# A gated linear attention followed by a squared-ReLU MoE: units of 256 tokens with two adjacent tokens per partition

## The chip, the cores and the metric

The kernel runs on one core of a Trainium2 chip. The metric is the device time of one execution in microseconds (us), lower is better. The kernel before was given at 212.42 us (median of 3, 212.36 to 215.28). Every later comparison runs both kernels in the same rounds on the same chip, and its ratio uses runs in the fast state alone.

## The reference, cut to what matters

```python
# B, H, S, D = 4, 8, 768, 48; q, k, v, alpha: [B, H, S, D] fp32, alpha in [0.8, 1.0]
for t in range(S):
    state = alpha[:, :, t, :, None] * state + einsum('bhd,bhe->bhde', k[:, :, t], v[:, :, t])
    y[:, :, t] = einsum('bhd,bhde->bhe', q[:, :, t], state)
x = y.transpose(0, 2, 1, 3).reshape(B * S, H * D)      # 3072 tokens x 384
h = x @ w_in                                           # 384 x 2048
out = maximum(h, 0) ** 2 @ w_out                       # 2048 x 384, fp32
```

Both kernels compute the recurrence in blocks: a cumulative sum of log(alpha) inside the block (a matmul with a triangular matrix), exponentials that scale k and q, transposes of the scaled k and q, masked scores between tokens of the block, products of the scores with v, and one state per batch entry that is carried from block to block. Then y is transposed and goes through the two layers.

Of the kernel before, what the change touches and what calls it, by code (L numbers as in the profile page):

```python
# [11 lines left out]
class Op:  # L12


    __slots__ = ("eng", "fn", "cost", "prio", "deps", "idx", "lag", "sem", "start", "end", "pos", "name",
                 "users", "ndeps", "alts")

    def __init__(self, eng, fn, cost, prio, name):
        self.eng, self.fn, self.cost, self.prio, self.name = eng, fn, cost, prio, name
        self.deps = {}  # L20
        self.lag = 0
        self.sem = None
        self.users = []
        self.pos = None


class Program:


    HOP = 90  # L30

    def __init__(self, nc):
        self.nc = nc
        self.ops = []
        self.writer = {}
        self.readers = {}
        self.dma_sems = {}
        self.dma_count = {}

    def add(self, eng, fn, cost, prio, reads=(), writes=(), name="", dma=None, lag=0, after=()):  # L40
        op = Op(eng, fn, cost, prio, name)
        op.idx = len(self.ops)
        op.lag = lag
        if dma is not None:
            if dma not in self.dma_sems:
                self.dma_sems[dma] = self.nc.alloc_semaphore("d_" + dma)
                self.dma_count[dma] = 0
            self.dma_count[dma] += 1
            op.sem = (dma, self.dma_count[dma])
        for o in after:  # L50
            op.deps[o] = True
        for k in reads:
            w = self.writer.get(k)
            if w is not None:
                op.deps[w] = True
            if k[0] == "ps":
                for r in self.readers.get(k, ()):
                    if r.eng != eng:
                        op.deps[r] = True
        for k in writes:  # L60
# [3 lines left out]
            for r in self.readers.get(k, ()):  # L64
                if r is not op:
                    op.deps.setdefault(r, r.eng != eng or r.sem is not None)
# [9 lines left out]
    def schedule(self):  # L76

        import heapq
# [4 lines left out]
        free = {}  # L83
        ready = {}
# [3 lines left out]
        for op in self.ops:  # L88
            free.setdefault(op.eng, 0.0)
            ready.setdefault(op.eng, [])  # L90
            if op.ndeps == 0:
                heapq.heappush(events, (0.0, seq, "r", op))
                seq += 1
        avail = {e: [] for e in free}
        order = {e: [] for e in free}
        done = 0
        now = 0.0
        while done < len(self.ops):
            t, _, kind, op = heapq.heappop(events)
            now = t  # L100
            batch = [(kind, op)]
            while events and events[0][0] <= now + 1e-9:
                _, _, k2, o2 = heapq.heappop(events)
                batch.append((k2, o2))
            for k2, o2 in batch:
                if k2 == "r":
                    heapq.heappush(avail[o2.eng], (o2.prio, o2.idx, o2))
            for e in avail:
                while avail[e] and free[e] <= now + 1e-9:
                    _, _, o = heapq.heappop(avail[e])  # L110
                    o.start = now
                    o.end = now + o.cost
                    free[e] = o.end
                    o.pos = len(order[e])
                    order[e].append(o)
                    done += 1
                    land = o.end
                    if o.sem is not None:
                        dma_free = max(dma_free, o.end + 1100) + o.lag
                        land = dma_free + 800  # L120
                    for u in o.users:
                        u.ndeps -= 1
                        hop = self.HOP if u.deps[o] else 0
                        u.start = max(getattr(u, "start", 0.0) or 0.0, land + hop)
                        if u.ndeps == 0:
                            heapq.heappush(events, (max(u.start, now), seq, "r", u))
                            seq += 1
                    heapq.heappush(events, (free[e], seq, "f", o))
                    seq += 1
        self.order = order  # L130
        self.makespan = max(o.end for o in self.ops)

    def place(self):

# [12 lines left out]
        for o in seq:  # L147
            kn = known.setdefault(o.eng, {})
            want = {}
            for d, sync in o.deps.items():  # L150
                if not sync or (o.eng == "pe" and d.eng == "pe" and d.sem is None):
# [6 lines left out]
            ds = sorted(want.values(), key=lambda d: -d.start)  # L158
            mine = []
            for d in ds:  # L160
# [14 lines left out]
        for e, ops in self.order.items():  # L175
# [9 lines left out]
    def emit(self, handles):  # L185
# [28 lines left out]
def pe_ns(*cols):  # L214
    return sum(max(n / 2.4 + 3, 27) for n in cols)


def act_ns(n):
    return 190 + n * 0.8333


def dve_ns(n, rate=1.0):
    return 135 + n / 0.96 / rate


def bass_gla_recurrent__then__act_relu_squared_kernel(
# [13 lines left out]
    C = 128  # L240
    NCH = S // C
# [3 lines left out]
    DP = 64  # L245
    G = B * NCH
    chunks = [(b, c) for c in range(NCH) for b in range(B)]

    NRAW, NLAB, NASB, NQKS, NKQT, NPM, NV, NXB, NRR, NGT, NOSB = 5, 2, 3, 3, 3, 2, 4, 2, 4, 6, 3
# [4 lines left out]
    RAW = sb("raw", [128, 4, HD], FP32, NRAW)  # L254
    LAB = sb("lab", [128, H, DP], BF16, NLAB)
    ASB = sb("asb", [128, 2, HD], BF16, NASB)
    QKS = sb("qks", [128, 2, H, DP], BF16, NQKS)
    KQT = sb("kqt", [128, 2, NPR, 128], BF16, NKQT)
    PM = sb("pm", [128, 2, NPR, 128], BF16, NPM)
    VBF = sb("vbf", [128, HD], BF16, NV)  # L260
    SBD = sb("sbd", [128, HD], BF16, B)
    TMP = sb("tmp", [128, HD], FP32, 2)
    ACM = sb("acm", [128, 2 * NPR], FP32, 2)
    XBF = sb("xbf", [128, HD], BF16, NXB)
    XT = nc.alloc_sbuf_tensor("xt", [128, KT, G * C], BF16)
    LTRI = nc.alloc_sbuf_tensor("ltri", [128, 128], BF16)
# [3 lines left out]
    HCOL = nc.alloc_sbuf_tensor("hcol", [128, 2 * NPR], BF16)  # L270
    WIN = nc.alloc_sbuf_tensor("win", [128, KT, DFF], BF16)
    WOUT = nc.alloc_sbuf_tensor("wout", [128, FT, DM], BF16)
    GT = sb("gt", [128, FT, 2 * C], BF16, NGT)
    RR = sb("rr", [128, 512], BF16, NRR)
    OSB = sb("osb", [128, DM], FP32, NOSB)

    psH = [nc.alloc_psum_tensor(f"psH{i}", [128, 512], FP32) for i in range(2)]
    psP = nc.alloc_psum_tensor("psP", [128, 2, 512], FP32)
    psO = nc.alloc_psum_tensor("psO", [128, 512], FP32)
    psA = nc.alloc_psum_tensor("psA", [128, 512], FP32)  # L280
    psT = nc.alloc_psum_tensor("psT", [128, 1024], BF16)
    psY = nc.alloc_psum_tensor("psY", [128, 512], FP32)
# [3 lines left out]
    P = 7000.0  # L286
# [9 lines left out]
    def fill(buf, val):  # L296
        return lambda e: e.memset(buf[:], val)

    def select(buf, op, fill_v, base, pattern, mult):
        return lambda e: e.affine_select(out=buf[:], in_=buf[:], compare_op=op, fill=fill_v, base=base,  # L300
                                         pattern=pattern, channel_multiplier=mult)

    for i, t in enumerate(LAB):
        add("dve", fill(t, 0.0), 300, -1e6, writes=[("lab", i)])
    for i, t in enumerate(QKS):
        add("dve", fill(t, 0.0), 600, -1e6, writes=[("qks", i)])
    add("pool", fill(LTRI, 1.0), 200, -1e6, writes=[("ltri",)])
    add("pool", select(LTRI, ALU.is_ge, 0.0, 0, [[1, 128]], -1), 300, -1e6, reads=[("ltri",)], writes=[("ltri",)])
    add("pool", fill(ONES2, 1.0), 100, -1e6, writes=[("ones",)])

    for buf, key in ((HSEL, "hsel"), (HCOL, "hcol")):
        add("dve", fill(buf, 0.0), 100, -2e6, writes=[(key,)])
    for part, key, val in ((HSEL[0:1, 64:128], "hsel", -1000.0), (HSEL[32:33, 0:64], "hsel", -1000.0),
                           (HCOL[0:1, 0:2 * NPR:2], "hcol", 1.0), (HCOL[32:33, 1:2 * NPR:2], "hcol", 1.0)):
        add("dve", lambda e, part=part, val=val: e.memset(part, val), 100, -2e6, reads=[(key,)], writes=[(key,)])

    add("pool", fill(IDENT, 0.0), 200, -1e6, writes=[("ident",)])
    add("pool", select(IDENT, ALU.not_equal, 1.0, 0, [[-1, 128]], 1), 300, -1e6, reads=[("ident",)],
        writes=[("ident",)])
    for i in range(B):  # L320
        add("pool", fill(SBD[i], 0.0), 400, -1e6 + 1, writes=[("sbd", i)])
# [4 lines left out]
    WQ = 2  # L326
    FQ = FT // WQ

    def w_in_dma(i):
        src = moe_w_in.rearrange("(kk p) n -> p kk n", p=128)[:, :, i * FQ * 128:(i + 1) * FQ * 128]  # L330
        return lambda e: e.dma_start(WIN[:, :, i * FQ * 128:(i + 1) * FQ * 128], src)

    def w_out_dma(i):
        src = moe_w_out.rearrange("(kk p) n -> p kk n", p=128)[:, i * FQ:(i + 1) * FQ, :]
        return lambda e: e.dma_start(WOUT[:, i * FQ:(i + 1) * FQ, :], src)

    raw_dma = {}
    wi_dma, wo_dma = {}, {}
    W_IN_AFTER = (0, "a")
    LOADS_HELD, W_OUT_AFTER = 1, 4  # L340

    def held(g):
        out = [wi_dma[0]] if g >= LOADS_HELD else []
        return out + ([wo_dma[0]] if g > W_OUT_AFTER else [])

    def attention(g):
        b, c = chunks[g]
        t0 = c * C
        p0 = g * P
        r, la, a, qs, kt, pm, vb, xb = (g % n for n in (NRAW, NLAB, NASB, NQKS, NKQT, NPM, NV, NXB))  # L350
        first, last = c == 0, c == NCH - 1

        for j, t, nm in ((3, alpha, "a"), (0, k, "k"), (1, q, "q"), (2, v, "v")):
            src = t[b, :, t0:t0 + C, :].rearrange("h p d -> p h d")
            dst = RAW[r][:, j, :].rearrange("p (h d) -> p h d", h=H)
# [214 lines left out]
```

## The kernel before: what the change and the argument touch

The kernel describes its work as operations with an engine, a cost, a priority and the buffers that they read and write. A small scheduler orders them per engine ahead of time, and waits on semaphores are derived from the buffers. All times in the code are plan costs in ns.

```python
C = 128                                   # tokens of a block ("chunk"); 24 chunks
RAW = sb("raw", [128, 4, HD], FP32, NRAW) # one token per partition
psA = nc.alloc_psum_tensor("psA", [128, 512], FP32)     # cumulative sums, alone in its bank
psT = nc.alloc_psum_tensor("psT", [128, 1024], BF16)    # every transpose
psY = nc.alloc_psum_tensor("psY", [128, 512], FP32)
...
for j, t, nm in ((3, alpha, "a"), (0, k, "k"), (1, q, "q"), (2, v, "v")):
    src = t[b, :, t0:t0 + C, :].rearrange("h p d -> p h d")       # pieces of 48 fp32 = 192 B
    dst = RAW[r][:, j, :].rearrange("p (h d) -> p h d", h=H)
...
dst = GT[gt][:, u * per:(u + 1) * per, 0:n]
eng, cost = ("pool", 1250) if u % 2 else ("dve", dve_ns(512, 2))  # squares: fixed alternation
...
add("sp", lambda e, ob=ob, r0=r0: e.dma_start(out[r0:r0 + C, :], OSB[ob][:]), 70, ps_ + 1300,
    reads=[("osb", ob)], name=f"out{g}", dma=f"o{ob}", lag=600)   # 128 rows of 1,536 B
```

All loads, outputs and (after the change) transposes by DMA are issued by SyncE into one queue; only the weights go through GpSimd's.

## Time and profile before

| | before |
|---|---|
| time, median | 212.42 us |
| TensorE busy share of the span | 85% |
| the busiest other engines (VectorE, ScalarE) | 52% |
| first 52 us | TensorE busy 24.6 us, DMA share 1.00 (179 GB/s) |
| from 52 us to the end | TensorE busy, nearly without a gap |
| last TensorE end to the end of the span | 209.8 to 212.6: 2.8 us |

The prediction below shows the page, the stretches and the timeline of this kernel. One more view matters later, the page's count of DMA packets and its list of DMA issues. The columns of the list are what was moved, the queue, the number of transfers, the size of one, and the median time in us from issue to landing.

```profile
DMA packets 106197, 27.04 MB, mean 127 GB/s; under 512 B 100288, under 2 KB 105408, under 8 KB 106176
...
raw<-in_k_dram SPq DMA_DIRECT2D x24, 192.0 KB, 3.7
...
raw<-in_alpha_dram SPq DMA_DIRECT2D x24, 192.0 KB, 3.6
out_dram<-osb SPq DMA_DIRECT2D x24, 192.0 KB, 2.3
```

A load of 192 KB lands after 3.6 to 3.7 us, and an output of the same size after 2.3 us.

### The profile page before, as it was taken

The numbers are of one execution on the slowest core, as the hardware profiler recorded it, in microseconds if no ns is written. First come the engines' busy times: TensorE is split into PE (matmuls) and PEld (weight loads), VectorE is DVE, ScalarE is ACT, GpSimd is POOL, SyncE is SP. The second block draws the span as 40 slices with busy tenths as digits, with TensorE's granted clock in tenths as the row PEclk, the third lists the DMA queues.
The fourth block names the chain that finished last, engine by engine and source line by source line (L and its number), as shares of the span: only waits on it lengthen the run. The fifth ranks groups of instructions, "written<-read, shape, count | busy, mean of one in ns | idle before, by whom it ended". The sixth has DMA issues, their size and how long they took to land.

```text
span 212.6 us, 4663 instructions
## 1 busy us (share of the span) xinstructions
PE 180.8 (85%) x1940; PEld 136.0 (64%) x1940; DVE 111.0 (52%) x175; ACT 111.5 (52%) x237; POOL 85.8 (40%) x105
## 2 busy tenths in 40 slices
PE   0346271677999999999999999999999999999984
PEld 0236151565776787777876877868778777677752
DVE  4151360345545767487677555675665655833200
ACT  2204230450665587574675585765756857374540
POOL 4403600140442296282564552735626615033330
PEclk9999855576999999999999999999999999999999
DMA  7499999999989987847907839365041010110101
GB/s 140 61 190 210 215 181 194 194 207 197 215 183 194 232 169 160 187 109 153 223 18 174 181 60 221 92 142 122 3 111 40 0 40 37 39 40 0 40 37 74
DMA packets 106197, 27.04 MB, mean 127 GB/s; under 512 B 100288, under 2 KB 105408, under 8 KB 106176
## 3 DMA queue, kind: packets, MB, share of 16 engines
q1 hardware_dynamic: 103296, 23.60, 51.7%
q0 software_dynamic: 2880, 3.15, 9.5%
q8 instruction: 15, 0.25, 0.4%
q14 instruction: 6, 0.05, 0.1%
HBM read 25.17 MB, written 4.72 MB: 141 GB/s over the span
## 4 chain that ended last, share of the span: by engine, by line
PE 77%; DMA 11%; SPq 6%; DVE 3%; ACT 1%; issue 1%
PE psO L512 30%; PE psH L490 29%; DMA raw<-in_alpha_dram 7%; SPq L356 6%; PE psT L396 4%; DMA win<-in_moe_w_in_dram 4%; PE psP L408 4%; PE psY L424 2%; PE psT L459 2%; PE psA L364 2%; PE psY L421 2%; PE psY L437 1%; DVE qks L386 1%; PE psA L368 1%; ACT osb L519 1%
## 5 line engine op out<-in xcount | busy, mean ns | idle before, releaser
L500 POOL TENSOR_TENSOR gt<-rr 128x512 bf16<-128x512 bf16 x48 | 51.4, 1072 | 73.2 <-ACT rr L496 73.2
L496 ACT ACTIVATE rr<-psH 128x512 bf16<-128x512 f32 x96 | 57.3, 597 | 45.0 <-PE psH L490 43.0
L490 PE MATMUL psH<-xt,win 128*128 128x256 bf16 (+1 forms) x624 | 78.3, 275 | 0.5 <-DMA win<-in_moe_w_in_dram 0.4
L512 PE MATMUL psO<-wout,gt 128*128 128x384 bf16 x384 | 77.6, 330 | 0.7 <-ACT osb L519 0.6
L490 PEld LDWEIGHTS psH<-xt,win 128*128 128x128 bf16 x624 | 58.3, 103 | 10.7 <-issue 0.8
L512 PEld LDWEIGHTS psO<-wout,gt 128*128 128x128 bf16 x384 | 34.0, 98 | 17.8 <-ACT osb L519 1.2
L413 DVE TENSOR_TENSOR pm<-psP,ltri 128x1024 bf16<-128x1024 f32 x24 | 29.3, 1221 | 14.2 <-PE psP L408 13.9
L500 DVE TENSOR_TENSOR gt<-rr 128x512 bf16<-128x512 bf16 x48 | 24.1, 503 | 21.2 <-ACT rr L496 20.7
L386 DVE TENSOR_TENSOR qks<-raw,asb 128x768 bf16<-128x768 f32 x24 | 24.6, 1024 | 17.1 <-ACT asb L377 17.1
L383 POOL CAST vbf<-raw 128x384 bf16<-128x384 f32 x24 | 13.4, 557 | 35.1 <-PE psY L437 18.1
L465 DVE COPY xt<-psT 128x384 bf16<-128x384 bf16 x24 | 8.6, 357 | 28.9 <-PE psT L459 28.9
L364 PE MATMUL psA<-lab,ltri 128*128 128x384 bf16 x24 | 8.4, 349 | 16.4 <-ACT lab L360 16.4
L360 ACT ACTIVATE lab<-raw 128x384 bf16<-128x384 f32 x24 | 12.7, 528 | 17.9 <-DMA raw<-in_alpha_dram 17.9
L402 DVE COPY kqt<-psT 128x1024 bf16<-128x1024 bf16 x24 | 16.5, 689 | 9.5 <-PE psT L396 9.1
L396 PE MATMUL psT<-ident,qks 128*128 128x128 bf16 x192 | 15.7, 229 | 4.7 <-DVE qks L386 4.4
L453 POOL TENSOR_TENSOR sbd<-tmp,acm 128x384 bf16<-128x384 f32 x16 | 15.8, 986 | 8.8 <-DVE tmp L451 8.8
L431 ACT ACTIVATE xbf<-psY 128x384 bf16<-128x384 f32 x24 | 11.8, 493 | 12.8 <-PE psY L424 12.8
L375 ACT ACTIVATE asb<-psA 128x384 bf16<-128x384 f32 x24 | 11.7, 489 | 11.7 <-PE psA L368 10.7
L396 PEld LDWEIGHTS psT<-ident,qks 128*128 128x128 bf16 x192 | 12.8, 102 | 7.2 <-DVE qks L386 5.0
L519 ACT ACTIVATE osb<-psO 128x384 f32<-128x384 f32 x24 | 11.8, 492 | 10.6 <-PE psO L512 10.5
L364 PEld LDWEIGHTS psA<-lab,ltri 128*128 128x128 bf16 x24 | 2.4, 98 | 17.7 <-ACT lab L360 17.1
L408 PE MATMUL psP<-kqt 64*128 64x128 bf16 x192 | 10.2, 230 | 2.6 <-DVE kqt L402 2.6
(36 smaller groups left out, 112.8 us busy)
## 6 DMA issues: line engine op xcount, KB each, us to landing
raw<-in_k_dram SPq DMA_DIRECT2D x24, 192.0 KB, 3.7
raw<-in_q_dram SPq DMA_DIRECT2D x24, 192.0 KB, 3.7
raw<-in_v_dram SPq DMA_DIRECT2D x24, 192.0 KB, 3.7
raw<-in_alpha_dram SPq DMA_DIRECT2D x24, 192.0 KB, 3.6
out_dram<-osb SPq DMA_DIRECT2D x24, 192.0 KB, 2.3
win<-in_moe_w_in_dram POOLq DMA_DIRECT2D x2, 768.0 KB, 9.3
wout<-in_moe_w_out_dram POOLq DMA_DIRECT2D x2, 768.0 KB, 11.3
```

The costliest lines, as they stand in the source:

```text
L364: ins = pe.matmul(psA[:, 0:HD], LTRI[:], lab)
L386: add("dve", lambda e: e.tensor_tensor(QKS[qs][:, :, :, 0:D], RAW[r][:, 0:2, :].rearrange("p j (h d) -> p j h d", h=H), ASB[a][:, :, :].re ...
L396: ins = pe.matmul(psT[:, o:o + 128], QKS[qs][:, j, 2 * p:2 * p + 2, :].rearrange("p h d -> p (h d)"), IDENT[:], is_transpose=True)
L402: add("dve", lambda e: e.tensor_copy(KQT[kt][:].rearrange("p j n s -> p (j n s)"), psT[:, :]), dve_ns(1024, 2), p0 + 3000, reads=[("ps", " ...
L408: ins = pe.matmul(psP[:, h, p * 128:(p + 1) * 128], KQT[kt][64 * h:64 * h + 64, 0, p, :], KQT[kt][64 * h:64 * h + 64, 1, p, :])
L413: add("dve", lambda e: e.tensor_tensor(PM[pm][:].rearrange("p j n s -> p (j n) s"), psP[:, :, :].rearrange("p j (n s) -> p (j n) s", n=NPR ...
L453: add("pool", lambda e: e.tensor_tensor(sb3, TMP[g % 2][:].rearrange("p (n d) -> p n d", d=D), acm, ALU.mult), 1100, p0 + 8000, reads=[("t ...
L490: ins = pe.matmul(psH[hb][:, i * n:(i + 1) * n], WIN[:, kk, fj * 128:(fj + 1) * 128], XT[:, kk, g0 * C:g0 * C + n], start=(kk == 0), stop= ...
L496: add("act", lambda e, hb=hb, rb=rb: e.activation(RR[rb][:], psH[hb][:], AF.Relu), act_ns(512), pu + 600, reads=[("ps", "H", hb)], writes= ...
L500: add(eng, lambda e, rb=rb, dst=dst: e.tensor_tensor(dst, RR[rb][:].rearrange("p (i s) -> p i s", i=per), RR[rb][:].rearrange("p (i s) -> ...
L512: ins = pe.matmul(psO[:, 0:DM], GT[gt][:, fj, ti * C:(ti + 1) * C], WOUT[:, fj, :], start=(fj == 0), stop=(fj == FT - 1))
L519: add("act", lambda e, ob=ob: e.activation(OSB[ob][:], psO[:, 0:DM], AF.Copy), act_ns(DM), ps_ + 700, reads=[("ps", "O")], writes=[("osb", ...
```

## The change

The intent is to shorten the starved start (larger DMA pieces, fewer logarithms, dummy matmuls on zeros that are to keep the clock up), and to take work from TensorE (transposes of the later units by DMA). Each partition now holds two adjacent tokens, so a load piece is 384 B. The product of the two alphas is taken first, and one logarithm serves the pair. The scheduler may now choose between engines for several operations. The diff is long; this is its core, with cuts marked.

```diff
-    C = 128
-    NCH = S // C
+    T = 256
+    NST = S // T
...
+    PE_TRANSPOSED = 6          # units 0 to 5 transpose on TensorE, 6 to 11 by DMA
+    PE_X = 6
+    AHEAD = 1                  # a unit's front is given priority one unit early
...
-    psP = nc.alloc_psum_tensor("psP", [128, 2, 512], FP32)
-    psA = nc.alloc_psum_tensor("psA", [128, 512], FP32)
-    psT = nc.alloc_psum_tensor("psT", [128, 1024], BF16)
-    psY = nc.alloc_psum_tensor("psY", [128, 512], FP32)
+    psX = nc.alloc_psum_tensor("psX", [128, 2, 512], FP32)
+    psZ = nc.alloc_psum_tensor("psZ", [128, 2, 512], FP32)
+    psW = nc.alloc_psum_tensor("psW", [128, 512], FP32)
...
-            src = t[b, :, t0:t0 + C, :].rearrange("h p d -> p h d")
+            src = t[b, :, t0:t0 + T, :].rearrange("h (p j) d -> p h (j d)", j=2)
...
+        add("dve", lambda e: e.tensor_tensor(hd(PRD[la][:]), al(0), al(1), ALU.mult), dve_ns(HD), p0,
+            reads=[("raw", r, 0)], writes=[("prd", la)], name=f"pr{g}",
+            alts={"pool": (lambda e: e.tensor_tensor(...), pool_ns(HD))})
...
+                ins = pe.matmul(psW[:, 0:HD], (LINC if incl else LSTR)[:], LAB[la][:, :, 0:D])
...
+                add("sp", lambda e, dst=dst, src=src: e.dma_start_transpose(dst, src), 500, p0 + 2500 + a,
+                    reads=[("qks", qs, a)], writes=[("kqt", kt, a)], name=f"tr{a}_{g}", dma=f"t{a}_{kt}", lag=1100)
...
+        if g < PE_X:
+            bank = as_bf16(psW)
+            def xtr(pe): ...   # 6 transposes of xbf into bank
+            add("pe", xtr, pe_ns(6, 128), p0 + 6700, reads=[("xbf", x2), ("ident",)], writes=[("ps", "W")],
+                name=f"xt{g}")
...
-            r0 = b * S + c * C
-            add("sp", lambda e, ob=ob, r0=r0: e.dma_start(out[r0:r0 + C, :], OSB[ob][:]), 70, ps_ + 1300,
+            r0 = b * S + i * T + 128 * jq
+            dst = bass.AP(tensor=out.tensor, offset=out.offset + r0 * DM, ap=[[DM, 2], [2 * DM, 64], [1, DM]])
+            add("sp", lambda e, ob=ob, dst=dst: e.dma_start(dst, OSB[ob][:]), 400, ps_ + 1300,
...
+    ORDER = ["f0", "f1", "b0", "b1", "f2", "b2", "f3", "f4", "b3"]     # fronts and backs of units
+    for g in range(5, G):
+        ORDER += [f"f{g}", f"b{g - 1}"]
...
+    pr.fill(lambda pe: pe.matmul(psO[:, 0:512], ZERO[:, 0:128], ZERO[:], skip_group_check=True), 216,
+            min(o.start for o in pr.order["pe"] if o.name.startswith("s2_")), 300, zero)
```

Two of these lines will matter most. The first is the output's access pattern. The rows of an output tile now lie in the order even tokens, odd tokens, so the pattern on the DRAM side has three dimensions, and the outermost has size 2. The second is that the cumulative sums of a unit (its "front") and the later transposes of another unit (its "back") write the same PSUM bank, psW.

## The prediction

> **What bounds the kernel now.** I read the page first, then stretches of ten microseconds, then the timeline. The page, with its slices (5.3 us each) and its chain that ended last:
>
> ```profile
> span 212.6 us, 4663 instructions
> PE 180.8 (85%) x1940; PEld 136.0 (64%) x1940; DVE 111.0 (52%) x175; ACT 111.5 (52%) x237; POOL 85.8 (40%) x105
> ...
> PE   0346271677999999999999999999999999999984
> ...
> PEclk9999855576999999999999999999999999999999
> DMA  7499999999989987847907839365041010110101
> ...
> PE 77%; DMA 11%; SPq 6%; DVE 3%; ACT 1%; issue 1%
> ```
>
> TensorE carries 77% of the chain, no other compute engine exceeds 52%, and everything on the chain that isn't TensorE sits early: PE is 0 to 7 tenths busy in the first ten slices and 9 afterwards. So there are two regimes. The stretches (us, busy time, instructions, clock, DMA share, GB/s) give the border:
>
> ```profile
> 20.00:30.00 10.00, 3.49 (x42) 2.43 (x43) 4.20 (x5) 3.89 (x10) 3.81 (x5) 0.75 1.14 199
> 30.00:40.00 10.00, 3.32 (x34) 2.66 (x33) 1.57 (x3) 1.08 (x3) 0.51 (x1) 0.50 1.16 187
> ...
> 52.40:210.00 157.60, 156.19 (x1687) 116.76 (x1685) 91.44 (x140) 96.29 (x204) 72.86 (x79) 1.00 0.50 111
> ```
>
> After 52.4 us PE is busy 156.2 of 157.6 us at full clock: pure TensorE throughput. Before it the DMA engines are full (share over 1), the compute engines are nearly idle, and the clock falls to half. The timeline shows what was waited for and how densely matmuls issue later:
>
> ```profile
> 31.40 6.04 SPq L356 DMA_DIRECT2D raw<-in_q_dram  x1
> ...
> 38.70 0.52 ACT L360 ACTIVATE lab<-raw 128x384 bf16<-128x384 f32 x1 [9.30 <-DMA raw<-in_alpha_dram]
> ...
> 133.68 1.47 PE L490 MATMUL psH<-xt,win 128*128 128x256 bf16 x12
> 135.08 0.40 PE L408 MATMUL psP<-kqt 64*128 64x128 bf16 x8
> 135.41 1.48 PE L490 MATMUL psH<-xt,win 128*128 128x256 bf16 x12
> 136.73 0.33 PE L364 MATMUL psA<-lab,ltri 128*128 128x384 bf16 x1
> ```
>
> A page's "mean ns" of a matmul (273) includes latency. The pitch is what counts: 135.41 to 136.73 is 1.32 us for 12 matmuls of 256 columns, 109 ns each. From starts in the same stretch: 384 columns 162 ns, 128 columns 56 ns, 96 columns 41 ns, anything under about 50 columns 25 ns. Score matmuls (64 rows) start in pairs 3 ns apart, one pair per 57 ns, so both row halves run together; around them the array stands for 95 ns on each side.
>
> Per 128 tokens before: the two MoE layers 24 x 109 + 16 x 162 = 5.21 us; cumulative sum 0.30; transposes 8 x 56 = 0.45; scores 4 x 57 + 2 x 95 = 0.42; state and intra products 0.17 + 0.21; state update 0.17; later transposes 0.17. Sum 7.10 us. The chain's L490 bursts return every 14.2 us for 256 tokens (133.84, 148.04, 162.24), exactly two of these. Over 24 chunks that is 170.4 us, less 1.9 for what first and last chunks skip: 168.5. So 44 of 212.6 us are no array work at full speed: about 40 in the first 52 us, 2.8 after the last matmul, 1 waiting for the last psO eviction.
>
> [...]the 98,304 packets of 192 B took 15.7 ns each (96 us over 16 engines, 196 GB/s), the 1,536 B output packets 65.5 ns (375 GB/s). [...]
>
> **The change part by part**, per unit of 256 tokens on TensorE.
> - Cumulative sums: one with the state extras (0.16 + 5 x 0.025) and one strict (0.16): 0.45 instead of 0.60.
> - Scores: 32 matmuls of 128 columns, four 64x64 tiles at once: 8 x 57 = 0.46, the same array time as before (two at once over twice the rows). No gain. Two groups, each with a switch in and out: 0.38, as before.
> - Intra products 16 pairs x 25 ns = 0.40 (before 0.42), state 8 x 41 = 0.33 (0.34) and update 0.33 (0.34) are unchanged in time, since halves run in pairs. But they now change mode too: 4 x 95 = 0.38 more.
> - First transposes 16 x 56 = 0.90 and later ones 0.34: unchanged in units 0 to 5, gone from PE in units 6 to 11 (-1.24).
> - MoE 10.42, unchanged.
>
> So units 0 to 5 cost 14.2 - 0.15 + 0.38 = 14.4 us, units 6 to 11 13.2. Sum 6 x 14.4 + 6 x 13.2 = 165.6, less 1.9 for what first and last units skip: 163.7 against 168.5. The steady state gains only 5 us.
>
> Other engines, per unit, by durations from the page. ScalarE: one logarithm 0.53, three exponentials 1.47, the small one 0.19, eight relus 4.78, two evictions of 0.49 and a wide one of about 0.83: 8.8. VectorE: scaling 2 x 1.02, masks 2 x 1.22, two state additions 1.10 and half of the squares 2.0: 7.6, plus about 1.9 for evictions in units 0 to 5. GpSimd: four products of 0.99, one cast of about 1.0, half of the squares 4.3: 9.2. All under 13.2, so none becomes the bound on average, but with less slack than before; a dependency chain of a unit stays hidden while the front is built one unit ahead.
>
> Startup, the larger part. Adjacent tokens make load pieces of 384 B. A line through 192 B at 15.7 ns and 1,536 B at 65.5 ns puts 384 B at 22.8 ns (an estimate): 272 GB/s, and 5.8 us for one 256-token unit (4 x 1,024 pieces) instead of 8.0 for two chunks. The weights took 9.6 (win) and 10.4 us (wout) of all engines and stay. First data at 2.4 us, then units 0 and 1 (11.6) and both weights (20.0): all landed by 34 us, unit 2's alpha by about 36. One unit's chain from alpha to xt is the product 0.55, log 0.53, sums 0.7, exponentials 1.5, scalings 2.0, transpose and eviction 1.7, score and two masks 2.9, products 0.7, evictions 2.0, transpose 0.5, and some sixteen handovers of about 0.1: 15 us. MoE of unit 2 can start near 52 us. Until then PE has units 0 and 1 complete (28.4) and the attention of unit 2 (3.6): 32 of 52 us, 20 lost, against 40 before. The dummy matmuls on zeros until the first second-layer matmul keep the clock up, so that the work there costs its full-speed price; before it cost nearly double from 25 to 45.5 us. One thing runs against this: while wout moved before (27 to 36 us), the 192 B loads got only 5 to 37 GB/s. Unit 1 may be starved in the same way behind win; loads of units 2 and on are now held until wout parts land, so unit 2 comes at about the same time and I charge 2 us.
>
> Tail: the same psO handover and output, 3.8, plus about 0.5.
>
> Sum: 163.7 + 20 + 2 + 4.3 = 190. A scheduler which fits the measured pitches (its switch cost is the 95 ns seen here) probably spends some of unit 2's latency on unit 3's front: I take 188.
>
> **Rivals.**
> (a) Small tiles cost more than their column count: [...]32 score weights and 16 state weights of 64 columns might queue one behind another at about 50 ns (an estimate: half the 97 ns recorded for a load). 32 x 50 - 460 = 1.1 us per unit and 0.4 for state: 18 us, total near 206. Against it: row-tiled weight loads in the old trace start 4 ns apart and overlap.
> (b) DMA transposes as the bound. They enter a single in-order queue on SyncE with the loads and outputs. At 4 us each, three per unit, they'd come to 12 us beside 13.2 and delay xt and kqt: 5 to 10 us more, total 193 to 198. For it: SPq issues already took 6 us when the queue was full. Against it: from unit 6 on the loads are almost done (DMA share under 0.3 from 150 us).
> (c) Static choice of engines and thinner buffers (XBF, EK, EQ, LAB two each) make PE wait where it never did: each 0.5 us per unit is 6 us, total 194.
> (d) Startup better than reckoned: 184 to 181, if unit 2's front overlaps well and weights beat my line.
>
> **Range and chances.** The floor is the 163.7 of array work plus about 13 of unavoidable start and 4 of tail, 181. (b) and (c) together reach 199, (a) 206. To miss 2% (208.2) two rivals have to come true at once. I say 188, 181 to 199; faster 0.94, same 0.04, slower 0.02.
>
> **What would show it.** Right: 4-tile groups pitched at 57 ns; load packets near 23 ns; the clock at full from a few us on; PE dense from about 30 to 35 us instead of 52; total PE pitch of a late unit about 13.2 us. Wrong: weight loads of the score tiles one behind another (a), PE idle released by DMA xt or kqt in the second half (b), PE idle released by VectorE, ScalarE or GpSimd after 60 us (c), or the first MoE block still starting after 40 us because unit 1's loads starve.

## The result, and the profile after

| | before | after |
|---|---|---|
| median, same rounds | 213.85 us (212.36 to 215.51, 4 runs) | 221.76 us (220.89 to 221.82, 4 runs) |
| ratio of fast runs, 95% interval | | 1.037 (1.029 to 1.045): slower |
| span of the profiled run | 212.6 us | 220.1 us |
| last TensorE end to the end of the span | 2.8 us | 9.2 us |

A ratio here is the mean time of one kernel's fast runs over that of the other's of the same rounds, so it is not quite the ratio of the medians. The prediction was 188 us, with 181 to 199. The kernel came out slower by 3.7%, so both the range and the direction were wrong.

The page of the changed kernel, its busy times, slices (5.5 us each) and chain:

```profile
span 220.1 us, 5346 instructions
...
PE 192.9 (88%) x2317; PEld 130.2 (59%) x2317; DVE 135.5 (62%) x214; ACT 101.7 (46%) x186; POOL 58.4 (27%) x72
...
PE   7999999998984998799319999999999999999830
...
PEclk9999999999998599999965999999999999999995
DMA  6997699999466679556979983457915650400110
...
PE 63%; DVE 13%; DMA 13%; SPq 3%; issue 2%; ACT 2%; DVEq 0%
```

TensorE is busy from the first slice (partly with dummy matmuls) and the clock is full (granted 1.0) from 5.5 us to the first dip, as intended. (The first record of the clock in this trace is at 5.5 us. The PEclk digits before a trace's first record are filled in and not measured: until 5.5 us the dummies start 427 ns apart, afterwards 216.) New are two dips, near 70 us and from 107 to 118 us, where PE falls to 4, 3 and 1 tenths and the clock to 0.5 (from 70.4 to 77.2 and from 111.3 to 121.6 us), and the last slices, 8, 3 and 0. TensorE's share of the chain fell from 77% to 63%, and VectorE's rose from 3% to 13%.

The stretches give the same in numbers. The columns are length, then the busy time and instructions of PE, PEld, DVE, ACT and POOL, then the granted clock, the DMA share and GB/s:

```profile
0.00:52.40 52.40, 49.81 (x569) 29.86 (x570) 38.18 (x61) 22.21 (x40) 23.10 (x37) 1.00 0.99 224
52.40:104.00 51.60, 45.14 (x604) 31.83 (x603) 39.94 (x60) 26.93 (x53) 18.23 (x18) 0.93 0.68 186
104.00:130.00 26.00, 17.97 (x192) 11.78 (x191) 11.12 (x18) 9.66 (x20) 5.66 (x6) 0.80 0.94 154
```

Before, PE was busy for 156.2 of the 157.6 us after 52.4. Now it is idle 8 of the 26 us from 104 to 130 alone, and that with a DMA share of 0.94 and only 154 GB/s: the DMA engines are occupied, but they move little.

Busy time also counts latency (a matmul of L658 is 274 ns long on the page, and they start 109 ns apart) and dummies. For a balance I counted each matmul by its steady pitch at full clock (the prediction's pitches). Everything else, dummies, waits, a low clock and the stops of about 95 ns where the tile shape changes (in the kernel before 93 and 94 ns around the scores at 135.1 us), is time without array work:

| time without array work, us | before | after |
|---|---|---|
| 0 to 52 us | 39.2 | 24.1 |
| 52 to 130 us | 4.1 | 25.0 |
| 130 us to the last TensorE end | 3.4 | 6.1 |
| from there to the end of the span | 2.8 | 9.2 |
| array work in the whole span | 163.1 | 155.7 |
| sum: the span | 212.6 | 220.1 |

So the start did win 15 us and the array work shrank by 7, and 21 us were given back between 52 and 130 us, 3 later on and 6 at the end.

The list of DMA issues answers to the one shown of before (loads are 384 KB now, twice as large):

```profile
raw<-in_alpha_dram SPq DMA_DIRECT2D x12, 384.0 KB, 6.0
...
out_dram<-osb SPq DMA_DIRECT2D x24, 192.0 KB
...
kqt<-qks SPq DMA_TRANSPOSE x12, 4.4
```

The output line has lost its landing time: the program could not pair issues with landings. The packet records say why. Outputs are packets of 1,536 B, 128 to a store. In the kernel before, the 128 packets of a store start within 0.6 to 2 us (the first store's within 3.4), and up to 21 of this size are in flight at once. In the changed kernel those of one store are spread over 3.9 to 4.9 us, there are never more than 4 in flight, and the last four stores lie back to back from 200.1 to 218.4 us. A single packet took nearly as long as before (mean 70.7 ns, before 65.5). 64 packets of 65.5 ns one after another are 4.2 us. This is what two DMA engines with 64 packets each would give. The profile does not name the engine of a packet, so "two" is inferred from this and from the pattern of the store; e9 below adds a count that says the same.

The end of the timeline (start, length, engine, line, operation, in brackets the idle time before it and what ended it):

```profile
210.93 0.49 ACT L690 ACTIVATE osb<-psO 128x384 f32<-128x384 f32 x1 [2.87 <-PE psO L683]
```

The last tile leaves PSUM at 211.4 us, and the span ends at 220.1. The 8.7 us between are stores that are still queued.

And the dip at 107 to 118 us:

```profile
108.35 0.99 POOL L447 TENSOR_TENSOR prd<-raw 128x384 f32<-128x384 f32 x1 [8.33 <-DMA raw<-in_alpha_dram]
109.30 1.04 POOL L673 TENSOR_TENSOR gt<-rr 128x512 bf16<-128x512 bf16 x1
110.48 0.81 PE L683 MATMUL psO<-wout,gt 128*128 128x384 bf16 x4 [3.85 <-POOL gt L673]
115.47 0.64 PE L573 MATMUL psX<-kqt 64*64 64x128 bf16 x16 [4.18 <-DMA kqt<-qks]
```

A late load of alpha holds GpSimd for 8.33 us. GpSimd works in its fixed order, so a square that was ready stands behind it. TensorE waits 3.85 us for this square, and a little later 4.18 us for a transpose by DMA. This is why a late DMA for another unit reaches TensorE. SyncE, which issues all of these in order, is held up too: it took 4.95 us to issue one transpose at 104.1 us, and 27.5 us for all twelve transposes `kqt<-qks`, where in e1 below it took at most 2.14 and in total 17.0 us.

### The profile page after: what moved, and what is told of

It is laid out like the page before. It is cut to its first block, busy times and chain, and to the rows that moved or that the text cites. A ratio compares the mean times of both kernels' runs of the same rounds, so it can differ in the third digit from the quotient of the medians.

```text
span 220.1 us, 5346 instructions
## 1 busy us (share of the span) xinstructions
PE 192.9 (88%) x2317; PEld 130.2 (59%) x2317; DVE 135.5 (62%) x214; ACT 101.7 (46%) x186; POOL 58.4 (27%) x72
## 4 chain that ended last, share of the span: by engine, by line
PE 63%; DVE 13%; DMA 13%; SPq 3%; issue 2%; ACT 2%; DVEq 0%
PE psO L683 27%; PE psH L658 22%; DMA xt<-xbf 5%; DMA raw<-in_q_dram 5%; DVE qks L490 3%; PE psX L600 3%; SPq L429 3%; DVE gt L671 3%; DMA kqt<-qks 3%; PE psX L593 2%; PE psO L725 2%; DVE kqt L511 2%; DVE pm L579 2%; PE psZ L573 1%; PE psZ L535 1%
## 5 line engine op out<-in xcount | busy, mean ns | idle before, releaser
L658 PE MATMUL psH<-xt,win 128*128 128x256 bf16 x576 | 73.5, 274 | 1.5 <-ACT rr L665 1.1
L658 PEld LDWEIGHTS psH<-xt,win 128*128 128x128 bf16 x576 | 54.2, 98 | 13.2 <-ACT rr L665 2.1
L671 DVE TENSOR_TENSOR gt<-rr 128x512 bf16<-128x512 bf16 x80 | 39.7, 506 | 33.3 <-ACT rr L665 32.8
L673 POOL TENSOR_TENSOR gt<-rr 128x512 bf16<-128x512 bf16 x16 | 19.2, 1204 | 43.7 <-ACT rr L665 43.3
L690 ACT ACTIVATE osb<-psO 128x384 f32<-128x384 f32 x23 | 11.3, 490 | 30.7 <-PE psO L683 30.4
L485 POOL CAST vbf<-raw 128x768 bf16<-128x768 f32 x12 | 10.9, 912 | 41.5 <-DMA raw<-in_v_dram 26.7
L725 PE MATMUL psO<-zero 128*128 128x512 bf16 x73 | 20.0, 414 | 1.3 <-DVE zero L360 1.3
L579 DVE TENSOR_TENSOR pm<-psX,caus 128x1024 bf16<-128x1024 f32 x12 | 14.6, 1213 | 8.1 <-PE psX L573 8.1
L610 ACT ACTIVATE xbf<-psX 128x768 bf16<-128x768 f32 x12 | 9.7, 810 | 19.9 <-PE psX L600 19.9
L579 DVE TENSOR_TENSOR pm<-psZ,caus 128x1024 bf16<-128x1024 f32 x12 | 14.6, 1215 | 6.0 <-PE psZ L573 6.0
L490 DVE TENSOR_TENSOR qks<-raw,eq 128x768 bf16<-128x768 f32 x12 | 12.7, 1055 | 0.3 <-DMA raw<-in_q_dram 0.2
L490 DVE TENSOR_TENSOR qks<-raw,ek 128x768 bf16<-128x768 f32 x12 | 11.4, 954 | 0.2
```

The costliest lines, as they stand in the source:

```text
L485: add("pool", lambda e: e.tensor_copy(VBF[vb][:].rearrange("p h j d -> p (h j d)"), RAW[r][:, 3].rearrange("p h j d -> p (h j d)")), pool_ ...
L490: add("dve", lambda e, a=a, E=E: e.tensor_tensor(QKS[qs][:, a, :, :, 0:D], RAW[r][:, 1 + a].rearrange("p h j d -> p j h d"), E[la][:].rear ...
L579: add("dve", lambda e, hf=hf, psT=psT: e.tensor_tensor(PM[pm][:, hf].rearrange("p r n j t -> p (r n) (j t)"), psT[:, :, :].rearrange("p r ...
L610: add("act", lambda e: e.activation(XBF[x2][:], psX[:, :, 0:HD], AF.Copy), act_ns(2 * HD), p0 + 6100, reads=[("ps", "X", 0), ("ps", "X", 1 ...
L658: ins = pe.matmul(psH[hb][:, i * n:(i + 1) * n], WIN[:, kk, fj * 128:(fj + 1) * 128], mov, start=(kk == 0), stop=(kk == KT - 1))
L671: add("dve", lambda e, dst=dst, sq=sq: e.tensor_tensor(dst, sq, sq, ALU.mult), dve_ns(512, 2), pu + 1200, reads=[("rr", rb)], writes=[("gt ...
```

## The experiments

The first theory is that the stores are the cause: their pattern confines each to two DMA engines, which lengthens the tail and delays every load and transpose that shares those engines (S). Its rivals: the transposes by DMA are slow in themselves (T, the prediction's rival (b)); or the engine choice made by the scheduler, with GpSimd doing only 16 of the 96 squares, makes VectorE a bound (E, part of (c)). A second theory came out of the first runs: the shared bank psW ties each front to the end of an earlier unit. Every result is the median of 4 runs (all of them; the ratios use the fast ones alone). The kernel before ran at 214.5 to 214.7 us in all these rounds, and all results are correct unless it is said. Not all runs met on one chip: e1 to e4 shared their rounds, e5 to e8 theirs, and e9 to e12 theirs. One run each of e1, e2 and e11 fell in the slow state.

### e1: the stores on more engines

```diff
-            dst = bass.AP(tensor=out.tensor, offset=out.offset + r0 * DM, ap=[[DM, 2], [2 * DM, 64], [1, DM]])
+            halves = [bass.AP(tensor=out.tensor, offset=out.offset + (r0 + j) * DM, ap=[[2 * DM, 64], [1, DM]])
+                      for j in range(2)]
+            def store(e, ob=ob, halves=halves):      # each half adds 16; the waits ask for 32 per tile
+                e.dma_start(halves[0], OSB[ob][0:64, :]).then_inc(pr.dma_sems[f"o{ob}"], 16)
+                return e.dma_start(halves[1], OSB[ob][64:128, :])
```

The order of operations on every engine is unchanged; only the store is issued as two transfers of 64 rows.

> Edit: each output store of the changed kernel (one transfer whose outermost output dimension is 2) becomes two transfers of 64 rows each; everything else, the order of every engine included, is as in the changed kernel. Theory S (the stores run on two DMA engines only: 128 packets take 4.1 us, never more than 4 at once, and loads that are spread over all engines wait for those two): a store takes about 0.5 to 1 us, the 8.7 us from the last eviction to the end shrink to about 2.5, and the waits for late loads between 60 and 125 us shrink by some 8 to 12 us: 201 to 206 us. Rival T (DMA transposes are what delays the middle): only the tail goes, 213 to 215 us. Rival E (engine choices of the scheduler make VectorE and GpSimd block in order): the same, 213 to 215 us.

It ran at 207.95 us, ratio 0.965 (0.958 to 0.973), so 13.8 us below the changed kernel and 3.5% faster than the one before. Its slow run is left out of the ratio. The profiled span is 206.6 us. The outputs in its list of DMA issues:

```profile
out_dram<-osb SPq DMA_DIRECT2D x48, 96.0 KB, 2.2
```

A store's packets again start within 0.6 to 2.4 us with up to 21 in flight, and the landing time is back. The time without array work between 104 and 130 us went from 11.9 to 1.7 us. The stores are a cause, and the largest found so far. The dip near 70 us remained (9.2 us without array work or dummies from 52 to 78 us in both).

### e2 and e9: the same pattern in the kernel before

```diff
-            add("sp", ... e.dma_start(out[r0:r0 + C, :], OSB[ob][:]), 70, ps_ + 1300,
+ e2         ... e.dma_start(bass.AP(..., ap=[[64 * DM, 2], [DM, 64], [1, DM]]), OSB[ob][:]), ...
+ e9         ... e.dma_start(bass.AP(..., ap=[[DM, 2], [2 * DM, 64], [1, DM]]), OSB[ob][:]), ...
```

> Edit: the kernel before with its output rows written as an access pattern of 2 x 64 rows, the same bytes. Theory S: its stores go to two engines and take about 4.1 us instead of 0.5; the tail grows by 3.6 to 8 us and loads come later, but the kernel before keeps more loads ahead: 217 to 224 us. If the two dimensions are merged when the program is built, nothing changes (212 to 214 us, stores of 0.5 us) and the run says nothing.

e2 ran at 214.21 us, ratio 1.000 (0.992 to 1.008). This miss says nothing about the theory. In its trace up to 21 packets of a store are in flight, their starts cover 0.6 to 2.3 us, and its page counts 106,197 packets, all as in the kernel before. 64 x 384 elements is just the step of the outer dimension, so the two dimensions describe one contiguous run of rows, and evidently they were merged when the kernel was built. e9 repeats it with the changed kernel's pattern, which cannot be merged. Its rows land in the wrong order, so its result is wrong on purpose.

> Edit: the kernel before stores its rows with the changed kernel's own access pattern (2, then 64 rows of every second row), which cannot be merged; the result is wrong on purpose (rows are interchanged), the bytes and the packets are the same. Theory S: a store takes about 4.1 us on two engines instead of 0.5. The last one ends 3.6 us later and may queue behind the one before it, and loads up to 157 us slow down; TensorE has more loads ahead, so 217 to 224 us, slower than before by 2 to 4%. If stores cost only in the changed kernel: 212 to 215 us.

e9 ran at 224.24 us, ratio 1.046 (1.037 to 1.055). Nothing else differs from the kernel before: this one line costs 9.7 us. Its page, with the chain and the DMA issues:

```profile
span 223.2 us, 4663 instructions
...
DMA packets 105861, 27.04 MB, mean 121 GB/s; under 512 B 99952, under 2 KB 105072, under 8 KB 105840
...
PE 66%; DMA 17%; SPq 7%; DVE 3%; ACT 2%; issue 1%; ACTq 0%
...
raw<-in_k_dram SPq DMA_DIRECT2D x24, 192.0 KB, 5.7
...
raw<-in_alpha_dram SPq DMA_DIRECT2D x24, 192.0 KB, 4.7
out_dram<-osb SPq DMA_DIRECT2D x24, 192.0 KB
```

The count of packets is the best evidence for two engines. The bytes are the same, but there are 336 packets fewer, all of them of 4 B. In the kernel before the trace has 1,985 such packets, which is 16 for each of its 124 transfers (96 loads, 24 stores, 4 for the weights) and one more. 336 is 24 stores x 14: here a store has 2 of them instead of 16. The changed kernel and e1 differ in the same way: 1,457 and 2,177 such packets, and the 720 between them are 48 stores x 16 less 24 x 2. That each of these small packets stands for one engine at work is an inference; with it the count gives two engines.

The loads are the same as before in size and number, but land after 4.7 and 5.7 us instead of 3.6 and 3.7. DMA has 17% of the chain instead of 11%. TensorE ends at 215.3 instead of 209.8 us, and the tail is 7.9 instead of 2.8 us. About half of the cost (5.5 us, between the two profiled runs) is thus felt before TensorE is done, and half (5.1 us) in the tail. Most of the first half is not due to the later loads. 4.4 us of it lie in one stretch, from 104 to 117 us, where PE is busy 9.71 of 13 us (before 12.50):

```profile
106.52 0.49 ACT L519 ACTIVATE osb<-psO 128x384 f32<-128x384 f32 x1 [4.08 <-DMA out_dram<-osb]
...
107.56 1.77 PE L490 MATMUL psH<-xt,win 128*128 128x256 bf16 x12 [2.90 <-ACT rr L496]
```

ScalarE waits 4.08 us until a slow store has released one of the three output buffers, TensorE waits 2.90 us for ScalarE's next tile, and the clock is low afterwards (0.87 in this stretch). The waits of the kernel before list none of ScalarE for a store. So in e9 the stores cost by their own duration: by the buffers that they hold, and by the tail.

### e3 and e4: all transposes on TensorE again

```diff
-    PE_TRANSPOSED = 6
-    PE_X = 6
+    PE_TRANSPOSED = 12
+    PE_X = 12
```

e3 is this edit in the changed kernel, e4 the same with e1's stores.

> Edit: all transposes of the changed kernel on TensorE (12 units instead of 6), the stores left as they are; the scheduler builds another order. Theory S: TensorE gains 6 x 1.24 = 7.4 us of work, late loads stay: 220 to 228 us. Rival T: the 8.4 us of waits for DMA transposes around 110 us and 2.2 us of engine time per transpose go: 210 to 216 us. Rival E: 220 to 226 us.

> Edits of both: stores as two transfers of 64 rows and all transposes on TensorE. Theory S: 203 to 210 us, that is, with the stores mended the DMA transposes help or cost a few us only. Rival T: well below the run with mended stores alone (by 5 us or more). Rival E: 214 to 220 us.

e3 ran at 234.17 us, ratio 1.088 (1.082 to 1.095): 12.4 us slower than the changed kernel. e4 ran at 221.25 us, ratio 1.030 (1.024 to 1.035), 13.3 us slower than e1. Rival T falls: the transposes by DMA are a gain in both. But the gain is far more than the 7.4 us (6 units x 1.24) that the transposes cost TensorE. (In e3's profiled run 5.5 us of it is a late start: the first products of scores and v come at 29.4 us instead of 23.9, and 24.4 in e4. e3 and e4 differ in nothing but the stores, which begin after 54 us, so the late start is not theirs. In this run VectorE waits 3.6 us for a load of q before that, 0.2 in the changed kernel.) In e4 units 4 to 7 followed one another at 17.5, 16.4 and 16.3 us, where TensorE had 14.4 us of work for one (the later ones at 14.0 to 14.4), and units 2 to 4 at 19 to 21 us, nearly as in e1. Something that isn't TensorE's throughput held them. The transposes on TensorE write PSUM tiles here, the later ones psW (L622). This led to the second theory.

### e6 and e8: the choice of engines

```diff
 e6 (e1 and:)
-            add("dve", lambda e, ...: e.tensor_tensor(dst, sq, sq, ALU.mult), dve_ns(512, 2), ..., alts={"pool": ...})
+            add("pool" if u % 2 else "dve", lambda e, ...: e.tensor_tensor(dst, sq, sq, ALU.mult), ...)
 e8 (e1 and:) the two products of exponentials and alpha lose their alternative on VectorE
```

> Edit on top of the mended stores (208 us): squares alternate between VectorE and GpSimd as in the kernel before (48 and 48) instead of 80 and 16 by the scheduler's choice; the bank stays shared. Rival E: VectorE loses 32 x 0.5 = 16 us of work, the stalls between 52 and 104 us shrink, 199 to 204 us. Theory B: 206 to 210 us.

> Edit on top of the mended stores (208 us): the two products of a front are held on GpSimd (0.99 us each instead of 0.56 on VectorE). Rival E: VectorE loses 23 x 0.6 = 14 us of work, 201 to 205 us. Theory B: the front's chain gets about 0.9 us longer per unit, 208 to 212 us.

The choice in the changed kernel can be read in the groups of instructions. Behind the bar stand busy time in us and the mean of one in ns, then the idle time before them and what ended most of it:

```profile
L671 DVE TENSOR_TENSOR gt<-rr 128x512 bf16<-128x512 bf16 x80 | 39.7, 506 | 33.3 <-ACT rr L665 32.8
...
L673 POOL TENSOR_TENSOR gt<-rr 128x512 bf16<-128x512 bf16 x16 | 19.2, 1204 | 43.7 <-ACT rr L665 43.3
```

e6, with 48 squares on each engine, ran at 207.76 us (0.966; e1 207.95). e8 ran at 206.03 us, ratio 0.960 (0.953 to 0.967); its interval overlaps e1's, so its 1.9 us are not established. Rival E falls as a cause of the loss. VectorE has 80 of the squares, where I had assumed half, but ahead of their squares both engines stood idle for ScalarE's output (32.8 and 43.3 us), so neither was short of time for them, and moving 32 squares changed nothing. Both were tested with psW shared; whether the choice costs anything once the bank is mended was not tried.

### e5 and e7: the later transposes in another bank

In the trace of e1 the shared bank can be read in two sets of three lines, for unit 3 and for unit 5: the logarithm that the cumulative sum needs, the copy of an earlier unit's transposes out of psW, and the cumulative sum.

```profile
47.62 0.52 ACT L448 ACTIVATE lab<-prd 128x384 bf16<-128x384 f32 x1 [1.15 <-DVE prd L445]
...
55.54 0.56 DVE L628 COPY xt<-psW 128x768 bf16<-128x768 bf16 x1 [3.25 <-PE psW L622]
...
56.16 0.34 PE L453 MATMUL psW<-lab,linc 128*128 128x384 bf16 x1
...
62.52 0.52 ACT L448 ACTIVATE lab<-prd 128x384 bf16<-128x384 f32 x1
...
76.45 0.56 DVE L628 COPY xt<-psW 128x768 bf16<-128x768 bf16 x1 [0.36 <-PE psW L622]
...
78.72 0.33 PE L453 MATMUL psW<-lab,linc 128*128 128x384 bf16 x1
```

Unit 3's logarithm is done at 48.14 us, but its sum starts at 56.16, 0.06 us after the copy of unit 2. Unit 5's is done at 63.04 and its sum starts at 78.72, after the copy of unit 3 has ended at 77.01. In the order f2, b2, f3, f4, b3, f5, b4 the sum of unit 5 writes the bank that b3 used before, so whatever delays one unit's back delays a later unit's front, which is then late for its own back. (A logarithm at 69.10, which looks like the partner of the sum at 78.72 at first sight, is unit 6's: they are counted from the start.)

```diff
-            bank = as_bf16(psW)
+            bank = as_bf16(psX)
...
-            add("pe", xtr, ..., writes=[("ps", "W")], ...)
+            add("pe", xtr, ..., writes=[("ps", "X", 0)], ...)          # and the copy reads ("ps", "X", 0)
```

psX has just been read when these transposes come, since their input is y, which is evicted from psX. e5 is this edit on e1, e7 the same with all transposes on TensorE. The scheduler plans around the bank, so it also builds another order: from about 26 us on the traces of e1 and e5 differ in it on all four compute engines. The edit is thus the bank together with the order that it allows.

> Edit on top of the mended stores (208 us): the later transposes of units 0 to 5 write bank psX instead of psW, so that the cumulative sums of a later unit need not wait in psW for the earlier unit's xt. Theory B (the shared bank chains the units: each front begins only after the previous unit's xt is out, 18 to 21 us per unit instead of about 14): the gaps between the units' products at 53, 74 and 92 us shrink to 13 to 16 us; 200 to 204 us. Rival E (VectorE, which got 80 of 96 squares, is the bound between 46 and 74 us): the same work stays on VectorE, 206 to 209 us.

> Mended stores, the later transposes in psX, and all transposes on TensorE. Beside the same with psW (221 us): theory B says the period of a late unit falls from 16.3 to about 14.5 us and the time to 207 to 213 us; rival E says 219 to 222 us. Beside the run with psX and DMA transposes: it tells what the DMA transposes are worth, by TensorE's count 6 x 1.24 = 7.4 us.

e5 ran at 199.86 us, ratio 0.931 (0.924 to 0.937): 8.1 us below e1, and 7.9 below e6 of the same rounds. e7 ran at 207.02 us, ratio 0.964 (0.956 to 0.972): 14.2 us below e4, which has twice as many units with transposes in this bank. The page's first line and, in a second fence, two stretches of e5 with the columns of above:

```profile
span 198.1 us, 5358 instructions
```

```profile
52.40:104.00 51.60, 48.77 (x706) 35.02 (x704) 46.91 (x67) 29.90 (x57) 25.34 (x23) 1.00 0.91 234
104.00:130.00 26.00, 26.00 (x345) 18.53 (x343) 20.54 (x33) 14.48 (x27) 7.07 (x7) 1.00 0.49 104
```

From 104 to 130 us PE is busy throughout, where the changed kernel had 17.97 of 26.00. In the timeline unit 3's sum now follows its logarithm at once, ten microseconds before the copy of unit 2's transposes:

```profile
46.88 0.52 ACT L448 ACTIVATE lab<-prd 128x384 bf16<-128x384 f32 x1 [1.93 <-DVE prd L445]
...
47.46 0.34 PE L453 MATMUL psW<-lab,linc 128*128 128x384 bf16 x1 [0.59 <-ACT lab L448]
...
57.01 0.55 DVE L628 COPY xt<-psX 128x768 bf16<-128x768 bf16 x1
```

In the profiled runs e5 also started earlier than e1: unit 0's products come at 23.8 and 25.6 us (23.9 in the changed kernel), before the two orders part. So up to 1.8 of the 8.1 us may not be the bank's.

The difference of e7 and e5, 7.2 us, is what the transposes by DMA are worth once they aren't mixed up with the bank: the prediction had 6 x 1.24 = 7.4.

### e10: the bank alone

This is e5's edit with the changed kernel's stores.

> Edit: the later transposes in psX, stores left on two engines (the changed kernel was 221.8 us, stores mended 208.0, both mended 199.9). If the two causes add up: 213 to 215 us. If late loads hide behind the bank's chain or the reverse: 216 to 222 us.

Its order on every engine is that of e5. It ran at 224.26 us, ratio 1.048 (1.041 to 1.055): no gain at all over the changed kernel (221.76, whose interval overlaps). Its waits (engine and line, what ended the wait, us in total, times, the longest):

```profile
PE psH L658 <- DMA xt<-xbf: 8.0, 2, 7.8
...
PEld psX L573 <- DMA kqt<-qks: 6.9, 1, 6.9
```

With the bank mended TensorE arrives earlier at the transposes by DMA and waits there, 7.8 us for one and 6.9 for another. The packets of those transposes (256 B) took 46.5 ns on average, against 38.1 in the changed kernel and 24.5 in e5; the median is 18 in the changed kernel and in e5, so a minority of packets take long. The two causes are therefore not additive:

| median, us | sums and transposes share psW | transposes in psX | the bank alone |
|---|---|---|---|
| stores with outermost 2 | 221.76 | 224.26 (e10) | +2.5 |
| stores with outermost 64 | 207.95 (e1) | 199.86 (e5) | -8.1 |
| the stores alone | -13.8 | -24.4 | |

The start of the products of scores and v shows when each cause acts. These are the distances from one unit to the next, in us:

| from unit to unit | 1 to 2 | 2 to 3 | 3 to 4 | 4 to 5 | 5 to 6 | 6 to 7 | 7 to 8 | 8 to 9 |
|---|---|---|---|---|---|---|---|---|
| after | 21.7 | 20.3 | 19.4 | 7.0 | 26.1 | 14.9 | 11.0 | 12.1 |
| e1 (stores mended) | 21.7 | 20.9 | 18.1 | 8.5 | 15.1 | 14.7 | 11.0 | 11.9 |
| e10 (bank mended) | 25.5 | 13.4 | 12.9 | 12.2 | 22.1 | 25.6 | 11.1 | 12.1 |
| e5 (both) | 25.5 | 13.4 | 13.3 | 11.7 | 14.0 | 14.7 | 11.0 | 11.9 |

The bank is the 20 us of the units 2 to 4 and vanishes with it in e10 and e5. Part of this gain is given back: with the new order unit 2 comes 3.8 us later after unit 1, and without the bank's chain unit 5 no longer catches up (7.0 and 8.5 us from unit 4). The stores are the 22 to 26 us of the units 5 to 7, when transposes by DMA begin, and vanish with them in e1 and e5.

### e11 and e12: the dummies and the lead of the front

Both start from e5. e11 takes the dummy matmuls away (the call of `pr.fill`), e12 sets `AHEAD = 0.75` instead of 1, so that a unit's front gets less priority over the rest.

> Edit: both mended (199.9 us), without the dummy matmuls on zeros. If they matter by the clock, it is at half speed for the first units: with 5 us of work before 26 us and some 3 us of first-layer work until the clock is up, 202 to 206 us. If they only fill idle time, 199 to 201 us.

> Edit: both mended, and the front of a unit has the priority of three quarters of a unit ahead instead of one, so that it overtakes less of the back of the unit before on VectorE. If VectorE's order still costs some of the 6 us of waits between 26 and 104 us: 197 to 199 us. If not: 199 to 202 us.

e11 ran at 202.74 us, ratio 0.946 (0.938 to 0.954): the dummies are worth 2.9 us. Its slices show the slow start again, in the first fence. The other two have the first 18 matmuls of the first layer, in e11 and in e5:

```profile
PE   0165599999879989999999999999999999999980
```

```profile
28.59 3.58 PE L658 MATMUL psH<-xt,win 128*128 128x256 bf16 x18
```

```profile
26.77 2.35 PE L658 MATMUL psH<-xt,win 128*128 128x256 bf16 x18
```

So they matter by the clock: until 31.6 us, where e11's first record of the clock stands, its matmuls start 213 ns apart (e5: 109), although the PEclk digits of its page say 9 from the start.

e12 ran at 197.74 us, ratio 0.924 (0.917 to 0.930), the fastest of all, 7.6% below the kernel before. Its interval overlaps that of e5, so the last 2.1 us are likely but not established by the intervals.

## Why the prediction was wrong

**What held.** The load packets of 384 B took 23.4 ns on average (median 22) where the line gave 22.8. The clock is at full speed (granted 1.0) from 5.5 to 70.4 us, and the first matmul of the first layer runs at 26.7 us instead of in stops and starts until 52. Groups of four score tiles start 3 to 4 ns apart with a pitch of 56 ns, so rival (a), serial weight loads, did not come true. Array work is 155.7 us; with about 9 us for switches (12 units x 8 x 95 ns) this is 164.8, the sum of the steady state had 163.7. In e5 the last six units follow each other every 12.8 us on average (93.3 to 170.3 us), where 13.2 was predicted.

**Readings and sums of the prediction that were off.** It dates the low clock of the kernel before from 25 to 45.5 us. The clock was also low until 18.2 us: up to there matmuls of 128 columns start 107 ns apart, and 56 from there to 25 us. VectorE was busy 11.3 us per unit (135.5 / 12) and not 7.6 to 9.5; this is still under TensorE's 13.2. And rivals (b) and (c) together give 199 to 204, not 199, so the upper end of the range was set too low by its own numbers.

**The step that failed first** is "Tail: the same psO handover and output, 3.8, plus about 0.5." The output was not the same. The diff had the line `ap=[[DM, 2], [2 * DM, 64], [1, DM]]`, and I read it as a mere reordering of rows. The tail was 9.2 us, and the stores cost far more than the tail: 13.8 us in the changed kernel, 24.4 with the bank mended, and 9.7 in the kernel before, where nothing but this line was changed. The rest of the cost comes through late loads and transposes in the changed kernel, and through output buffers that come free late in e9. That a store with an outermost size of 2 runs on two engines is inferred from these runs, and none of them names an engine: 3.9 to 4.9 us for the packets of a store, against 64 x 65.5 ns = 4.2; at most 4 packets in flight, against 21 with an outermost size of 64 (e1) or 128 (before); and in e9 2 packets of 4 B for each store instead of 16. Other sizes were not run.

How a load or a transpose is delayed by the stores was seen only from outside: landings lengthened (3.6 to 4.7 us for alpha in e9), SyncE took longer to issue (27.5 us for the twelve transposes `kqt<-qks`, 17.0 in e1), and a minority of the transposes' packets took long (a mean of 38.1 ns at a median of 18; in e5 24.5). Two explanations fit and neither was shown: a load may be spread over 16 engines, as its 16 packets of 4 B suggest, and wait for its share on the two that the stores are inferred to use; or the slow stores hold up in the queue what SyncE issues next. No record of a single engine tells the two apart.

**The step that failed second** is "a dependency chain of a unit stays hidden while the front is built one unit ahead." I added up the busy time of each engine and concluded from the sums that nothing would stand still. But the front could not be built ahead: its cumulative sums and the later transposes of an earlier unit share psW, and the distance between units was 20 us where TensorE had 14.4. The kernel before kept the sums alone in psA. This is rival (c) in kind, but I had put it at 0.5 us per unit and looked for it in the engines and in SBUF buffers (XBF, EK, EQ, LAB), not in a bank. It cost 8.1 us once the stores were mended, and 14.2 with all transposes on TensorE.

Rival (b) came true in its sign ("PE idle released by DMA xt or kqt"), but not for its reason. Its 4 us for a transpose were my estimate, with no measured number behind it. The `kqt` transposes of 256 KB took 4.4 us in the median from issue to landing in the changed kernel, beside the slow stores, and 3.2 in e5; all transposes by DMA together are worth 7.2 us there.

**The sum, term by term**, with e5, in which both are mended. It has 155.5 us of array work and some 9 of switches, 164.6 against 163.7; a tail of 4.6 against 4.3; and 28.9 us of start and other waits against 22. So even without the two mistakes the sum of 190 would have been about 8 us short of e5's span of 198.1. The startup estimate is not at fault: up to 52 us e5 has 22.6 us without array work or switches, against 22. Some 6 to 7 us come after it, where the sum allowed none, nearly 5 of them between 52 and 104 us. In e12 this stretch has 2.4, but the one from 104 to 130 us has 2.2 instead of 0.5, so the priorities move these waits more than they remove them. The failed term is again the dependency chain that was to stay hidden. The median of e5 (199.9) lies just above the range and that of e12 (197.7) in it.

The chance of 0.02 for "slower" was wrong for a plain reason. It was derived from the rivals that I had thought of. Two lines that the stated change does not mention, the store's pattern and the bank of the later transposes, were on no list of mine.

What stays open is whether e10 is really 2.5 us slower than the changed kernel (other rounds, overlapping intervals), how much of the 8.1 us is the bank and how much the order built with it, and where the last 7 us between the sum and e5 lie one by one.

## What to carry to other kernels

When the layout of a tile changes, read every access pattern that touches it, the stores too: look at the size of the outermost dimension first (64 instead of 2 in the stores gained 13.8 us in e1), then at the size of the pieces (a packet of 192 B took 15.7 ns, one of 384 B 23.4). The signs of the slow stores here were a missing landing time in the list of DMA issues and at most 4 packets in flight instead of 21. Beside them loads of alpha landed after 4.7 us instead of 3.6, and ScalarE waited 4.08 us for an output buffer (both in e9). When buffers are merged, write down who must finish before whom in each PSUM bank: sums of busy time per engine cannot show a chain that goes through a bank.
